# A fused attention and MLP kernel: sums of exponentials by narrow products, the maximum of phi as a tree, q of four units transposed on the tensor engine, and low parts moved from VectorE to GpSimd

## The chip, the cores and the metric

The kernel runs on one core of a Trainium2 chip. The metric is the time of one execution in device microseconds (us), the median of three runs. Engines are called as the profile calls them: PE (the tensor engine's products; PEld its weight loads), DVE (VectorE), ACT (ScalarE), POOL (GpSimd) and SP (SyncE, which issues all transfers here).

## The reference

```
q, k, v: 4 x 8 x 576 x 64     phi: 4 x 8 x 576 x 32        (batch, heads, seq, dim)
a = exp(phi - max over seq);  a = a / (sum over seq + 1e-9)
k_m = a^T k;  v_m = a^T v                                   (32 x 64 per head)
scores = q k_m^T / 8;  attn = softmax over the 32
x = attn v_m, heads side by side                            (2304 x 512)
h = max(x w1, x w2, x w3);  x = h w_out                     (512 -> 768 -> 512)
y = x w_in;  out = softplus(y) w_out2                       (512 -> 2048 -> 512)
```

## The kernel before

Every float32 operand of a large product is split into a high part `hi` (the value cast to the matmul's float32r) and a low part `lo` (the value minus `hi`); a product is then three, hi·hi, lo·hi and hi·lo. The weights arrive as 64-bit floats, two 32-bit words each; the class `Conv` (lines 255 to 290) turns them into float32 with one ACT and two DVE steps, then makes `hi` by a cast and `lo` by a subtraction. `hi_eng` and `lo_eng` say on which engines; the defaults are ACT and POOL.

Attention goes by eight units `u`, each a batch and four heads. `load_phi` brings phi as 128 rows by 4 heads by 5 row groups by 32; the fifth group has only 64 rows, so its other 64 are filled (table `pad`). `att_max` (L349) reduces over the row groups on DVE, PE transposes the result, DVE takes the maximum over rows, PE spreads it. `att_exp` subtracts it and takes exponentials on ACT. `att_sum` (L371) adds `et` over the row groups on DVE; `sums` (L398) adds over rows by one product with ones, and its reciprocal `ri` scales k_m and v_m when ACT copies them out of PSUM (`kvd`). `att_x` multiplies `et` with k or v in twenty products of 32 output rows (L387, L389). `att_tr` turns k_m and v_m by products with selection matrices. `att_q` (L472) transposes q by one DVE instruction of 128 x 1152, in 32 x 32 blocks; a second form, on PE, is there for units named in `qpe`, which is empty. `att_sc` makes the scores, `att_sm0` to `att_sm2` the softmax, and `att_fin` turns the result back and splits it into `ah` and `al`.

The MLP follows: `u_mm` multiplies v_m with w1 to w3 (so x is never formed) and splits the result into `uh` and `ul`; `m1` multiplies by the attention weights and takes the maximum of three (L602 to L609); `hsplit` splits h into `hh` and `hlo` (table `hl` gives the engine of the low part); `m1out` multiplies by w_out (L643 to L645), 12 products of 384 columns for each split piece. `y0_split` splits the first half's result. All of this is done for two halves of the batch. The last stage (L863 to L908) does the second MLP.

What sets the order: `PLAN` is a list of steps for units 0 to 3 and the first weights; for the rest the table `C` gives the slot at which each step is written beside the main loop. From what is written, the framework's scheduler makes one fixed order for each engine; an engine takes its instructions strictly in that order. In the profile the plan runs to about 94 us, the first half's m1 to 174, its m1out to 222, the second half's m1 to 291 and its m1out to 343.

Of the kernel before, what the change touches and what calls it, by code (L numbers as in the profile page):

```python
# [165 lines left out]
def fused_kernel(ctx: ExitStack, tc: tile.TileContext, q, k, v, phi, w1, w2, w3, w_out, m_in, m_out, out):  # L166
# [201 lines left out]
    def att_sum(u):  # L368
        d = U[u]
        er = t_p.tile([P, 4 * M], F32, tag="mx", name="er", bufs=2)  # L370
        nc.vector.tensor_reduce(out=er, in_=d["et"].rearrange("p r c -> p c r"), op=ALU.add, axis=AX.X)  # L371
        d["er"] = er

    def att_x(u, i):
# [6 lines left out]
        if new_ri and u < 4:  # L381
            sums(u, pst()[:, 0:2])
        for r in range(R4 + 1):
            for h in range(4):
# [1 line left out]
                if r < R4:
                    nc.tensor.matmul(xp[a, 0:D], et[:, r, a], x[:, h, r], start=(r == 0), stop=False)  # L387
                else:
                    nc.tensor.matmul(xp[a, 0:D], et[0:SREM, r, a], xr[:, h], start=False, stop=True)  # L389
        if new_ri and u >= 4:  # L390
            sums(u, xp[:, 64:66])
# [3 lines left out]

    def sums(u, s):
        d = U[u]
        nc.tensor.matmul(s, d.pop("er"), ones, start=True, stop=True)  # L398
        ri = t_p.tile([P, 1], F32, tag="ri", name="ri", bufs=2)
        nc.vector.tensor_scalar(out=ri, in0=s[:, 0:1], scalar1=1e-9, scalar2=None, op0=ALU.add)  # L400
        nc.vector.reciprocal(out=ri, in_=ri)
        d["ri"] = ri
# [559 lines left out]
```

## Time and profile before

| | us |
|---|---|
| median of three runs (747.47 to 751.0) | 749.6 |
| the profiled execution | 749.13 |
| its span | 747.3 |
| busy: PE / DVE / ACT / POOL | 697.7 / 475.4 / 307.6 / 245.5 |

The span is the time from the first to the last instruction; the execution's own time is 1.8 us longer. Busy time is a sum over stretches with different limits, so the prediction goes by stretch. Ends of matmuls are modelled: a PE that is shown busy may still run below its peak.

### The profile page before, as it was taken

Reading aid. Unit: us, or ns where it says so; the run is one execution under the profiler, and the core shown is the slowest. Engines: PE = TensorE matmul, PEld = TensorE weight load, DVE = VectorE, ACT = ScalarE, POOL = GpSimd, SP = SyncE. Lnnn points to the kernel's source line nnn. Section 1 sums busy time; section 2 is a strip of 40 time slices with the busy share of each in tenths; the row PEclk is TensorE's granted clock in tenths of the full one; section 3 lists DMA queues with packets and bytes.
Section 4 is the critical chain, followed back from the end, with each engine's and each line's share of the span. In section 5 each row is a group of like instructions: output and inputs, shape, how many; then the busy total and the mean of one; then the engine's idle time right before and its main releaser. Section 6 shows DMA issues by size and latency. Waiting matters only on the chain. (4 is left out here: it accounts for less than half of the span.)

```text
span 747.3 us, 11707 instructions
## 1 busy us (share of the span) xinstructions
PE 697.7 (93%) x4380; PEld 628.2 (84%) x4380; DVE 475.4 (64%) x858; ACT 307.6 (41%) x645; POOL 245.5 (33%) x237
## 2 busy tenths in 40 slices
PE   2679799999989999998999999999999999999997
PEld 1457588889889999987899889898889899898896
DVE  7799978999978984882333487333784334433343
ACT  2256456644657763652333453222542223222221
POOL 1212301333675413642222363222552223422221
PEclk9979789999999999998999999999999999999999
DMA  9993703341252400540000032000241000011112
GB/s 291 289 305 123 222 13 109 120 131 54 78 162 85 128 1 7 165 146 24 1 1 1 7 127 93 0 1 1 64 133 30 1 1 0 1 43 42 43 43 84
DMA packets 52568, 59.21 MB, mean 79 GB/s; under 512 B 8992, under 2 KB 46368, under 8 KB 52512
## 3 DMA queue, kind: packets, MB, share of 16 engines
q1 hardware_dynamic: 52512, 58.47, 25.5%
q8 instruction: 34, 0.56, 0.3%
q14 instruction: 22, 0.18, 0.1%
HBM read 53.74 MB, written 4.72 MB: 78 GB/s over the span
## 5 line engine op out<-in xcount | busy, mean ns | idle before, releaser
L250 POOL TENSOR_TENSOR gl<-m,gh 128x384 fp32r<-128x384 f32 x96 | 100.4, 1047 | 259.3 <-ACT gh L242 242.6
L869 DVE TENSOR_SCALAR e<-pst 128x384 int32<-128x384 int32 x96 | 53.2, 554 | 138.7 <-PE pst L863 138.7
L871 ACT ACTIVATE L<-e 128x384 f32<-128x384 f32 x96 | 50.3, 524 | 188.2 <-DVE e L869 188.1
L895 PE MATMUL acc<-oh,gh 128*128 128x512 f32 x288 | 114.2, 396 | 0.4 <-ACT gh L242 0.4
L895 PE MATMUL acc<-ol,gh 128*128 128x512 f32 x288 | 113.8, 395 | 0.0
L863 PE MATMUL pst<-yb,ih 128*128 128x384 f32 x384 | 102.1, 336 | 0.0
L873 DVE SCALAR_TENSOR_TENSOR m<-pst,L 128x384 f32<-128x384 f32 x96 | 53.4, 556 | 57.9 <-ACT L L871 56.8
L602 PE MATMUL psm<-ah,uh 128*128 128x288 f32 x288 | 86.9, 312 | 2.7 <-ACT kT L436 1.7
L602 PE MATMUL psm<-al,uh 128*128 128x288 f32 x288 | 85.8, 299 | 0.0
L602 PE MATMUL psm<-ah,ul 128*128 128x288 f32 x288 | 84.3, 300 | 0.0
L895 PE MATMUL acc<-oh,gl 128*128 128x512 f32 x288 | 82.7, 394 | 0.0
L242 ACT ACTIVATE gh<-m 128x384 fp32r<-128x384 f32 x96 | 50.0, 523 | 62.8 <-DVE m L873 60.8
L863 PEld LDWEIGHTS pst<-yb,ih 128*128 128x128 f32 x384 | 70.0, 188 | 3.4 <-DVE m L873 0.7
L863 PE MATMUL pst<-y0h,ih 128*128 128x384 f32 x192 | 65.7, 342 | 3.9 <-DVE m L873 3.8
L863 PE MATMUL pst<-y0l,ih 128*128 128x384 f32 x192 | 65.3, 340 | 0.0
L863 PE MATMUL pst<-y0h,il 128*128 128x384 f32 x192 | 65.2, 340 | 0.0
L250 POOL TENSOR_TENSOR wl<-cg,wh 128x384 fp32r<-128x384 f32 x37 | 39.8, 1080 | 75.5 <-ACT wh L242 63.1
L863 PE MATMUL pst<-yb,il 128*128 128x384 f32 x192 | 64.4, 335 | 0.0
L895 PEld LDWEIGHTS acc<-oh,gh 128*128 128x128 f32 x288 | 54.3, 189 | 10.7 <-ACT gh L242 0.9
L895 PEld LDWEIGHTS acc<-oh,gl 128*128 128x128 f32 x288 | 53.6, 187 | 11.4
L895 PEld LDWEIGHTS acc<-ol,gh 128*128 128x128 f32 x288 | 54.3, 188 | 9.0
L602 PEld LDWEIGHTS psm<-ah,uh 128*128 128x128 f32 x288 | 54.7, 194 | 6.2 <-ACT kT L436 2.0
(142 smaller groups left out, 1410.9 us busy)
## 6 DMA issues: line engine op xcount, KB each, us to landing
wraw<-in_moe_w_dram SPq DMA_DIRECT2D x66, 256.0 KB, 3.6
raw<-in_moe_w_in_dram SPq DMA_DIRECT2D x16, 512.0 KB, 3.5
raw<-in_moe_w_out_dram SPq DMA_DIRECT2D x16, 512.0 KB, 3.6
qr<-in_q_dram SPq DMA_DIRECT2D x8, 576.0 KB, 4.6
out_dram<-o SPq DMA_DIRECT2D x18, 256.0 KB, 2.1
kvm<-in_k_dram SPq DMA_DIRECT2D x8, 512.0 KB, 7.9
kvm<-in_v_dram SPq DMA_DIRECT2D x8, 512.0 KB, 7.6
wor<-in_moe_w_out_dram SPq DMA_DIRECT2D x6, 512.0 KB, 3.5
```

Of the source, the lines that this page charges most:

```text
L242: nc.scalar.activation(out=dst, in_=src, func=AF.Copy)
L250: e.tensor_tensor(out=dst, in0=src, in1=hi, op=ALU.subtract)
L602: nc.tensor.matmul(x, l[:, t, ws], r[:, cs], start=(n == 0), stop=(n == 5))
L863: nc.tensor.matmul(hx, l[:, ds], r[:, cs], start=(n == 0), stop=(n == 3 * ND - 1))
L869: nc.vector.tensor_scalar(out=e.bitcast(I32), in0=hx.bitcast(I32), scalar1=0x7FFFFFFF, scalar2=None, op0=ALU.bitwise_and)
L871: nc.scalar.activation(out=L, in_=e, func=AF.Softplus, scale=-1.0)
L873: nc.vector.scalar_tensor_tensor(out=m, in0=hx, scalar=0.0, in1=L, op0=ALU.max, op1=ALU.add)
L895: nc.tensor.matmul(acc[0][t], l[:, t * P:(t + 1) * P], r, **kw)
```

## The change

Five edits. (1) `att_sum` and `sums` go; after the first of a unit's two sets of products, `att_x` issues twenty more with the same weights `et` and two columns of ones, into columns 64 and 65 of the same PSUM tile. (2) `att_max` takes maxima of halves in three two-input operations in place of one reduction. (3) `qpe` names units 0 to 3: q is loaded as k is, in two transfers, and transposed by 20 products with the identity, then copied out of PSUM by ACT; k_m is turned by two products in place of eight, and the scores are made by products of 64 output rows. (4) All tables of engines for high and low parts go: every `Conv` has its high part on ACT and its low part on POOL; all `hlo` but the first and last of a half are on POOL, and so are two more `al`. (5) The pad of phi is a POOL memset to 0, and the zero fill of `et` goes.

```diff
-    ('ca', 0, 1, {'lo_eng': 'pool', 'hi_eng': 'act'}),
-    ('ex', 0, 'dve'),
-    ('sm', 0),
+    ('ca', 0, 1),
+    ('ex', 0),
...
-    'esub': ['pool', 'pool', 'pool', 'dve'],
-    'wok': [{'hi_eng': 'act'}, {'lo_eng': 'dve', 'hi_eng': 'act'}, {'lo_eng': 'pool', 'hi_eng': 'dve'}, {'hi_eng': 'act', 'lo_eng': 'pool'}, {'lo_eng': 'pool', 'hi_eng': 'act'}, {'lo_eng': 'dve', 'hi_eng': 'dve'}],
-    'al': ['dve', 'dve', 'pool', 'dve'],
+    'al': ['pool', 'pool', 'pool', 'dve'],
-    'hl': ['pool', 'pool', 'dve', 'pool', 'pool', 'dve', 'dve', 'dve', 'pool', 'dve', 'dve', 'pool', 'dve', 'pool', 'pool', 'dve', 'dve', 'pool'],
+    'hl': ['dve'] + ['pool'] * 16 + ['dve'],
-    'qpe': (),
-    'pad': ['act', 'act', 'dve', 'act', 'act', 'act', 'dve', 'pool'],
-    'zed': ['dve', 'pool', 'dve', 'pool', 'pool', 'pool', 'dve', 'pool'],
+    'qpe': (0, 1, 2, 3),
...
-        cast(C["pad"][u], ph[SREM:P, :, R4, :], ph[SREM:P, :, 0, :])
+        nc.gpsimd.memset(ph[SREM:P, :, R4, :], 0.0)
...
-        nc.vector.tensor_reduce(out=mx, in_=d["ph"].rearrange("p h r m -> p h m r"), op=ALU.max, axis=AX.X)
+        ph = d["ph"]
+        m2 = t_p.tile([P, 4, 2, M], F32, tag="m2", name="m2", bufs=1)
+        nc.vector.tensor_tensor(out=m2, in0=ph[:, :, 0:2], in1=ph[:, :, 2:4], op=ALU.max)
+        nc.vector.tensor_tensor(out=mx, in0=m2[:, :, 0], in1=m2[:, :, 1], op=ALU.max)
+        nc.vector.tensor_tensor(out=mx[0:SREM], in0=mx[0:SREM], in1=ph[0:SREM, :, R4], op=ALU.max)
...
-        (nc.vector if C["zed"][u] == "dve" else nc.gpsimd).memset(et[SREM:P, R4], 0.0)
...
-        er = t_p.tile([P, 4 * M], F32, tag="mx", name="er", bufs=2)
-        nc.vector.tensor_reduce(out=er, in_=d["et"].rearrange("p r c -> p c r"), op=ALU.add, axis=AX.X)
...
+        if new_ri:
+            for r in range(R4 + 1):
+                for h in range(4):
+                    a = slice(32 * h, 32 * h + 32)
+                    k = slice(0, P if r < R4 else SREM)
+                    nc.tensor.matmul(xp[a, D:D + 2], et[k, r, a], ones[k], start=(r == 0), stop=(r == R4))
+            ri = t_p.tile([P, 1], F32, tag="ri", name="ri", bufs=2)
+            nc.vector.tensor_scalar(out=ri, in0=xp[:, D:D + 1], scalar1=1e-9, scalar2=None, op0=ALU.add)
+            nc.vector.reciprocal(out=ri, in_=ri)
...
-        nc.tensor.matmul(s, d.pop("er"), ones, start=True, stop=True)
...
-                nc.tensor.matmul(sc[64 * s:64 * s + 64, 0:HS], kT[:, s], qT[:, s, c * HS:(c + 1) * HS],
+                o = s ^ units[u][0] % 2
+                nc.tensor.matmul(sc[64 * s:64 * s + 64, 0:HS], kT[:, o], qT[:, o, c * HS:(c + 1) * HS],
                                  start=True, stop=True)
...
-                c = w_conv(i, p, **C["wk"].get((i, p), {}))
+                c = w_conv(i, p)
```

The scheduler's fixed orders move with it. On DVE at the start of the program, before (qT is the transposed q, mx and er the reductions, mc and md the maximum over rows, ph and et phi and its exponentials):

```order
L472 STREAM_TRANSPOSE qT<-qr 128x2x18x32
L349 TENSOR_REDUCE mx<-ph 128x128 x2
L472 STREAM_TRANSPOSE qT<-qr 128x2x18x32
L353 TENSOR_REDUCE mc<-psm 128x1 x2
L355 TENSOR_SCALAR md<-ident,mc 128x128 x2
L362 TENSOR_TENSOR ph<-ph,psm 128x640 x2
L365 MEMSET et 64x128
L371 TENSOR_REDUCE er<-et 128x128
```

and DVE at the same place with the change:

```order
L342 TENSOR_TENSOR m_128<-ph 128x256
L343 TENSOR_TENSOR mx<-m_128 128x128
L344 TENSOR_TENSOR mx<-mx,ph 64x128
L342 TENSOR_TENSOR m_140<-ph 128x256
L343 TENSOR_TENSOR mx<-m_140 128x128
L344 TENSOR_TENSOR mx<-mx,ph 64x128
L348 TENSOR_REDUCE mc<-psm 128x1
L350 TENSOR_SCALAR md<-ident,mc 128x128
L348 TENSOR_REDUCE mc<-psm 128x1
L350 TENSOR_SCALAR md<-ident,mc 128x128
L357 TENSOR_TENSOR ph<-ph,psm 128x640 x2
```

Nothing stands between the two maxima and the subtractions any more, and no sum follows them. On POOL at the end of the first half's m1out and after it, before (sT are steps of the softmax, al and hlo low parts of attention and of h, wl of weights, y0l of the first half's result):

```order
L250 TENSOR_TENSOR hlo<-h,hh 128x384
L250 TENSOR_TENSOR wl<-cg,wh 128x384 x2
L250 TENSOR_TENSOR hlo<-h,hh 128x384
L250 TENSOR_TENSOR y0l_2887<-ya,y0h_2886 128x384
L250 TENSOR_TENSOR y0l_3014<-ya,y0h_3013 128x384
L250 TENSOR_TENSOR y0l_3166<-ya,y0h_3165 128x384
L250 TENSOR_TENSOR y0l_3314<-ya,y0h_3313 128x384
L250 TENSOR_TENSOR wl<-cg,wh 128x384
L250 TENSOR_TENSOR hlo<-h,hh 128x384
L250 TENSOR_TENSOR wl<-cg,wh 128x384
```

and POOL there with the change:

```order
L503 TENSOR_TENSOR sT<-sT,ssm 128x576
L241 TENSOR_TENSOR al<-aT,ah 128x576
L241 TENSOR_TENSOR y0l_3117<-ya,y0h_3116 128x384 x3
L241 TENSOR_TENSOR y0l_3244<-ya,y0h_3243 128x384 x2
L241 TENSOR_TENSOR y0l_3396<-ya,y0h_3395 128x384 x2
L241 TENSOR_TENSOR y0l_3544<-ya,y0h_3543 128x384 x2
L241 TENSOR_TENSOR y0l_3244<-ya,y0h_3243 128x384
L241 TENSOR_TENSOR y0l_3396<-ya,y0h_3395 128x384
L241 TENSOR_TENSOR y0l_3544<-ya,y0h_3543 128x384
L241 TENSOR_TENSOR wl<-cg,wh 128x384 x2
L241 TENSOR_TENSOR hlo<-h,hh 128x384
```

The twelve low parts of the first half's result now stand in one piece, ahead of the next low parts of weights. On PE after the first unit's products, before (kvd is the scaled k_m or v_m, psm and pst are PSUM tiles):

```order
L428 MATMUL psm<-pick,kvd 32x128 x8
L351 MATMUL psm<-ident,mx 128x128
L485 MATMUL psm<-qT,kT 128x288 x4
L387 MATMUL psm<-kvm,et 32x64 x12
```

and PE there with the change (qn and qnr are q as loaded):

```order
L382 MATMUL psm<-ones,et 32x2 x20
L399 MATMUL psm<-pick_90,kvd 64x128 x2
L346 MATMUL psm<-ident,mx 128x128
L450 MATMUL psm<-ident,qn 64x128 x8
L453 MATMUL psm<-ident,qnr 64x64 x2
L450 MATMUL psm<-ident,qn 64x128 x8
L453 MATMUL psm<-ident,qnr 64x64
L351 MATMUL psm<-md,onesq 128x128
L453 MATMUL psm<-ident,qnr 64x64
L470 MATMUL psm<-qT,kT 64x288 x4
```

The sums and the transposes of q stand ahead of the first scores; the transposes of two more units follow before the first product of `u_mm`.

## Rows read from the trace of the kernel before

**Rows 1.** Busy time by stretch: PE, PEld, DVE, ACT, POOL, PEclk, DMA, GB/s.

```profile
0.00:42.00 42.00, 19.05 (x237) 13.04 (x238) 33.27 (x62) 11.85 (x26) 8.68 (x23) 0.99 1.06 295
42.00:94.00 52.00, 43.23 (x540) 33.16 (x540) 50.23 (x101) 26.70 (x63) 13.66 (x16) 0.83 0.70 205
94.00:174.00 80.00, 77.50 (x643) 69.54 (x644) 71.25 (x153) 45.23 (x109) 16.80 (x19) 0.97 0.32 99
174.00:222.00 48.00, 43.80 (x237) 42.28 (x236) 45.19 (x71) 25.75 (x54) 29.77 (x23) 0.96 0.29 94
222.00:291.00 69.00, 67.99 (x492) 67.56 (x492) 55.28 (x117) 43.74 (x102) 22.40 (x21) 1.00 0.18 58
291.00:343.00 52.00, 47.36 (x256) 45.33 (x256) 38.92 (x55) 28.68 (x55) 28.84 (x21) 0.96 0.38 122
343.00:747.00 404.00, 398.76 (x1983) 357.27 (x1981) 181.30 (x302) 125.59 (x238) 125.35 (x114) 1.00 0.10 33
```

**Rows 2.** Waits of PE over the span: total us, times, longest.

```profile
PE psm L351 <- DVE mx L349: 14.5, 3, 9.0
...
PE psm L643 <- DVE ul L585: 3.4, 1, 3.4
...
PE psm L645 <- POOL hlo L250: 1.0, 1, 1.0
```

**Rows 3.** Timeline of DVE: start, us; 0 to 105 and 190 to 215 us.

```profile
4.84 2.33 DVE L472 STREAM_TRANSPOSE qT<-qr 128x1152 f32<-128x1152 f32 x1 [1.28 <-DMA qr<-in_q_dram]
...
31.78 2.30 DVE L472 STREAM_TRANSPOSE qT<-qr 128x1152 f32<-128x1152 f32 x1
...
194.59 0.52 DVE L250 TENSOR_TENSOR hlo<-h,hh 128x384 fp32r<-128x384 f32 x1
...
197.43 1.37 DVE L250 TENSOR_TENSOR hlo<-h,hh 128x384 fp32r<-128x384 f32 x1
```

**Rows 4.** Groups of DVE to 222 us: busy, mean ns; idle before.

```profile
L371 DVE TENSOR_REDUCE er<-et 128x128 f32<-128x640 f32 x8 | 10.1, 1265 | 0.1
...
L349 DVE TENSOR_REDUCE mx<-ph 128x128 f32<-128x640 f32 x8 | 10.0, 1258 | 0.5 <-ACT ph L242 0.5
...
L250 DVE TENSOR_TENSOR hlo<-h,hh 128x384 fp32r<-128x384 f32 x9 | 8.1, 908 | 0.0
...
L250 DVE TENSOR_TENSOR wl<-cg,wh 128x384 fp32r<-128x384 f32 x7 | 3.8, 547 | 0.1
...
L250 DVE TENSOR_TENSOR wol<-cg,woh 128x256 fp32r<-128x256 f32 x4 | 1.6, 404 | 0.0
...
L246 DVE CAST wh<-cg 128x384 fp32r<-128x384 f32 x8 | 3.1, 390 | 0.0
...
L276 DVE SCALAR_TENSOR_TENSOR cg<-wraw,cg 128x384 int32<-128x384 int32 x31 | 21.1, 689 | 0.3
```

**Rows 5.** Groups of POOL to 222 us.

```profile
L250 POOL TENSOR_TENSOR wl<-cg,wh 128x384 fp32r<-128x384 f32 x22 | 23.2, 1061 | 57.8 <-ACT wh L242 45.3 <-DVE wh L246 7.6 <-DVE ri L400 2.8
...
L250 POOL TENSOR_TENSOR hlo<-h,hh 128x384 fp32r<-128x384 f32 x9 | 11.0, 1227 | 8.3 <-ACT hh L242 5.4 <-PE psm L485 1.8 <-PE psm L645 1.1
...
L250 POOL TENSOR_TENSOR y0l<-ya,y0h 128x384 fp32r<-128x384 f32 x8 | 10.9, 1389 | 0.0
```

**Rows 6.** Timeline of POOL, 190 to 215 us.

```profile
196.85 1.53 POOL L250 TENSOR_TENSOR hlo<-h,hh 128x384 fp32r<-128x384 f32 x1
```

**Rows 7.** Timeline of PE, 33 to 42 us; each product has two records.

```profile
33.16 0.65 PE L428 MATMUL psm<-pick,kvd 128*32 128x128 f32 x16 [0.43 <-ACT kvd L393]
...
34.31 2.21 PE L485 MATMUL psm<-qT,kT 128*128 128x288 f32 x8 [0.50 <-ACT kT L433]
...
36.66 0.65 PE L387 MATMUL psm<-kvm,et 128*32 128x64 f32 x32
...
40.03 0.44 PE L412 MATMUL psm<-pick,kvd 128*64 128x128 f32 x4
```

**Rows 8.** Groups of ACT to 222 us.

```profile
L242 ACT ACTIVATE wh<-cg 128x384 fp32r<-128x384 f32 x21 | 10.9, 521 | 10.3 <-DVE cg L276 7.5 <-PE psm L575 2.5
```

More of the change, by code (lines that the diff above doesn't have):

```diff
@@ L30 @@
     ('wl', 0, 0),
-    ('ca', 0, 1, {'lo_eng': 'pool', 'hi_eng': 'act'}),
-    ('ex', 0, 'dve'),
-    ('ex', 1, 'dve'),
-    ('sm', 0),
+    ('ca', 0, 1),
+    ('ex', 0),
+    ('ex', 1),
     ('ld', 0, 0),
-    ('sm', 1),
     ('ax', 0, 0),
-    ('ca', 0, 0, {'lo_eng': 'pool', 'hi_eng': 'dve'}),
+    ('ca', 0, 0),
     ('tr', 0, 0),
@@ L44 @@
     ('qT', 0),
-    ('ca', 0, 2, {'lo_eng': 'pool', 'hi_eng': 'dve'}),
+    ('ca', 0, 2),
     ('cb', 0, 0),
@@ L53 @@
     ('ld', 0, 1),
-    ('qT', 1, 'dve'),
+    ('qT', 1),
     ('tr', 1, 0),
@@ L60 @@
     ('ld', 3, 1),
-    ('ca', 0, 3, {'lo_eng': 'pool', 'hi_eng': 'act'}),
+    ('ca', 0, 3),
     ('mx', 3),
@@ L64 @@
     ('ax', 0, 1),
-    ('ex', 2, 'dve'),
+    ('ex', 2),
     ('s2', 0, 'pool'),
@@ L70 @@
     ('s0', 1),
-    ('ex', 3, 'pool'),
+    ('ex', 3),
     ('s1', 1, 'dve'),
@@ L77 @@
     ('wl', 1, 0),
-    ('ca', 1, 1, {'lo_eng': 'dve', 'hi_eng': 'dve'}),
+    ('ca', 1, 1),
     ('fin', 0, 'dve'),
@@ L83 @@
     ('u', 0, 3, (0,)),
-    ('sm', 2),
     ('s2', 1, 'pool'),
@@ L87 @@
     ('wl', 2, 0),
-    ('qT', 3, 'dve'),
+    ('qT', 3),
     ('ax', 2, 1),
-    ('ca', 1, 0, {'lo_eng': 'dve', 'hi_eng': 'act'}),
+    ('ca', 1, 0),
     ('wl', 2, 1),
-    ('ca', 1, 3, {'lo_eng': 'pool', 'hi_eng': 'dve'}),
-    ('sm', 3),
+    ('ca', 1, 3),
     ('wl', 3, 0),
@@ L105 @@
     ('tr', 3, 1),
-    ('ca', 1, 2, {'lo_eng': 'dve', 'hi_eng': 'act'}),
+    ('ca', 1, 2),
     ('u', 1, 1, (0, 1)),
@@ L109 @@
     ('u', 1, 3, (0, 1)),
-    ('ca', 2, 0, {'lo_eng': 'pool', 'hi_eng': 'act'}),
+    ('ca', 2, 0),
     ('u', 1, 0, (0, 1)),
     ('cb', 1, 2),
-    ('ca', 2, 1, {'lo_eng': 'pool', 'hi_eng': 'dve'}),
+    ('ca', 2, 1),
     ('u', 0, 1, (1,)),
@@ L122 @@
     ('m1', 1, 0, 0),
-    ('ca', 2, 3, {'lo_eng': 'pool', 'hi_eng': 'act'}),
+    ('ca', 2, 3),
     ('u', 0, 3, (1,)),
@@ L131 @@
     ('s0', 3),
-    ('ca', 2, 2, {'lo_eng': 'pool', 'hi_eng': 'act'}),
+    ('ca', 2, 2),
     ('cb', 2, 2),
@@ L154 @@
     'w8l': 17,
-    'wk': {(4, 0): {'hi_eng': 'act', 'lo_eng': 'dve'}, (4, 1): {'lo_eng': 'dve', 'hi_eng': 'act'}, (3, 0): {'hi_eng': 'dve', 'lo_eng': 'pool'}, (5, 3): {'lo_eng': 'pool'}, (3, 1): {'hi_eng': 'act', 'lo_eng': 'dve'}, (5, 0): {'hi_eng': 'dve', 'lo_eng': 'pool'}, (4, 2): {'lo_eng': 'pool'}, (3, 2): {'hi_eng': 'act', 'lo_eng': 'dve'}, (5, 1): {'lo_eng': 'pool', 'hi_eng': 'act'}, (5, 2): {'lo_eng': 'pool', 'hi_eng': 'act'}, (4, 3): {'hi_eng': 'dve', 'lo_eng': 'pool'}},
     'wo_off': {(4, 0): 1, (5, 3): 0, (5, 1): -1, (3, 3): -1, (3, 0): 0, (4, 1): -2, (3, 2): 0, (5, 0): -1, (3, 1): 1, (5, 2): -2, (4, 3): 0, (4, 2): 0},
-    'hl': ['pool', 'pool', 'dve', 'pool', 'pool', 'dve', 'dve', 'dve', 'pool', 'dve', 'dve', 'pool', 'dve', 'pool', 'pool', 'dve', 'dve', 'pool'],
+    'hl': ['dve'] + ['pool'] * 16 + ['dve'],
     'us0': 1,
     'us1': 0,
-    'qpe': (),
-    'pad': ['act', 'act', 'dve', 'act', 'act', 'act', 'dve', 'pool'],
-    'zed': ['dve', 'pool', 'dve', 'pool', 'pool', 'pool', 'dve', 'pool'],
+    'qpe': (0, 1, 2, 3),
 }
@@ L357, in att_max, with att_exp @@
         d["ma"] = st[:, P:2 * P].rearrange("p (h m) -> p h m", h=4)
-    def att_exp(u, sub="dve"):
+    def att_exp(u):
         d = U[u]
@@ L364, in att_exp @@
         nc.scalar.activation(out=et.rearrange("p r h m -> p h r m"), in_=ph, func=AF.Exp)
-        (nc.vector if C["zed"][u] == "dve" else nc.gpsimd).memset(et[SREM:P, R4], 0.0)
         d["et"] = et.rearrange("p r h m -> p r (h m)")
-    def att_sum(u):
-        d = U[u]
-        er = t_p.tile([P, 4 * M], F32, tag="mx", name="er", bufs=2)
-        nc.vector.tensor_reduce(out=er, in_=d["et"].rearrange("p r c -> p c r"), op=ALU.add, axis=AX.X)
-        d["er"] = er
     def att_x(u, i):
@@ L380, in att_x @@
         new_ri = "ri" not in d
-        if new_ri and u < 4:
-            sums(u, pst()[:, 0:2])
         for r in range(R4 + 1):
@@ L385, in att_x @@
                 a = slice(32 * h, 32 * h + 32)
[L386 to L391, printed above, removed]
+                k = slice(0, P if r < R4 else SREM)
+                nc.tensor.matmul(xp[a, 0:D], et[k, r, a], x[:, h, r] if r < R4 else xr[:, h], start=(r == 0), stop=(r == R4))
+        if new_ri:
+            for r in range(R4 + 1):
+                for h in range(4):
+                    a = slice(32 * h, 32 * h + 32)
+                    k = slice(0, P if r < R4 else SREM)
+                    nc.tensor.matmul(xp[a, D:D + 2], et[k, r, a], ones[k], start=(r == 0), stop=(r == R4))
+            ri = t_p.tile([P, 1], F32, tag="ri", name="ri", bufs=2)
+            nc.vector.tensor_scalar(out=ri, in0=xp[:, D:D + 1], scalar1=1e-9, scalar2=None, op0=ALU.add)
+            nc.vector.reciprocal(out=ri, in_=ri)
+            d["ri"] = ri
         kvd = t_p.tile([P, D], F32, tag="kvd", name="kvd", bufs=3)
@@ L394, in att_x @@
         d["xp", i], d["kvd", i] = xp, kvd
-    def sums(u, s):
-        d = U[u]
-        nc.tensor.matmul(s, d.pop("er"), ones, start=True, stop=True)
[L399 to L402, printed above, removed]
     def att_tr(u, i):
@@ L730, in fused_kernel @@
             nc.gpsimd.memset(x[:, 2 * s + 1 - s % 2].bitcast(F32), 0.0)
-    STEPS = dict(ph=load_phi, ld=load_x, q=load_q, mx=att_max, ex=att_exp, sm=att_sum, ax=att_x, tr=att_tr, qT=att_q,
+    STEPS = dict(ph=load_phi, ld=load_x, q=load_q, mx=att_max, ex=att_exp, ax=att_x, tr=att_tr, qT=att_q,
                  sc=att_sc, s0=att_sm0, s1=att_sm1, s2=att_sm2, fin=att_fin, wl=w_load, ca=conv_a, cb=conv_b,
@@ L752, in fused_kernel @@
         u = 4 + n
-        for sl, fn in zip(C["att"][n], (lambda u=u: att_max(u), lambda u=u: att_exp(u, C["esub"][u - 4]), lambda u=u: att_sum(u),
+        for sl, fn in zip(C["att"][n], (lambda u=u: att_max(u), lambda u=u: att_exp(u), lambda: None,
                                         lambda u=u: (att_kv(u), load_u(u + 2) if u + 2 < 8 else None),
@@ L759, in wo_go @@
         def wo_go(j=j):
-            wcv[j] = wo_conv(j, **C["wok"][j])
+            wcv[j] = wo_conv(j)
             wcv[j][0].a()
```

## The prediction

> **What bounds the kernel now.** I read three views: busy time by stretch, the waits of the tensor engine (PE), and the groups of instructions of the vector engine (DVE). By stretch [rows 1], the last 404 us are PE's alone: 398.8 us busy at a granted clock of 1.00, the other engines under half. The change touches nothing there, so the question is the first 343 us. From 42 to 222 us DVE is the fullest engine: 50.2 of 52, 71.3 of 80 and 45.2 of 48 us, 166.7 of 180 together, while PE leaves at least 8.8 + 2.5 + 4.2 = 15.5 us idle (a lower bound, since ends of matmuls are modelled) and is granted 0.83 of its clock in the 52 us after 42, where it ran in pieces. From 222 to 343 us PE leads again (68.0 of 69 us, then 47.4 of 52). The first 42 us are full of transfers: DMA share 1.06 at 295 GB/s, PE busy 19.1. The waits say the same: before the last stage PE waits longest for DVE's maximum of phi, 14.5 us in three waits, and then for a PSUM buffer that DVE had not yet read, 3.4 us in one [rows 2]. So work taken off DVE should help from 42 to 222 us, if nothing else takes its place.
>
> **What leaves DVE.** Four of eight transposes of q go: 4 x 2.32 = 9.3 us, all before 35 us (the first starts at 4.84, the fourth at 31.78 [rows 3]). Eight sums `er` go: 8 x 1.265 = 10.1 [rows 4]. Eight reductions `mx` of 1.258 become three maxima of 256, 128 and (64 partitions) 128 elements. The nearest row is a two-input operation of 256 elements, 0.404 us; at 0.40 + 0.27 + 0.23 = 0.90 (the shorter two are my estimate from it) the tree saves 8 x 0.36 = 2.9 us; at three times 0.404 it saves only 0.4, and if the shorter two cost 0.15 each, 4.4. Casts to ACT: 8 x 0.390 and 4 of 256 elements at about 0.28 (0.390 scaled by length) give 4.2. Low parts to POOL: 7 x 0.547 + 4 x 0.404 + 7 of the 9 `hlo` before 222 us at 0.908 + two `al` at about the same make 3.8 + 1.6 + 6.4 + 1.8 = 13.6. Five fills of pads and zeros go, put at 0.25 each (a cast of three times their length takes 0.390): 1.3. Sum: 9.3 + 10.1 + 2.9 + 4.2 + 13.6 + 1.3 = **41.4 us**, of which I place some 15 before 42 us (four transposes, a quarter of the sums, half the trees and fills, a fifth of the casts).
>
> **What the low parts cost on POOL.** There `wl` takes 1.061 and `hlo` 1.227 us [rows 5]: 7 x 1.06 + 4 x 0.7 + 7 x 1.23 + 2 x 1.4 = 21.6 us more POOL before 222 us, and 7 more `hlo`, 8.6 us, behind it. POOL has room on average (13.7 of 52, 16.8 of 80 us), least from 174 to 222 (29.8 of 48 [rows 1]). But DVE slows beside POOL. Within 3 us of one timeline the same `hlo` takes 0.52 us at 194.59, before POOL starts, and 1.37 at 197.43 [rows 3], beside a subtraction that POOL began at 196.85 and that took 1.53 [rows 6]. The means show how often: the conversion's 31 L276 average 0.689, against 0.547 for the equally long `wl`, and the nine `hlo` 0.908 against 0.52 [rows 3, 4]. That is 31 x 0.14 + 9 x 0.39 = 7.9 us for POOL's 68.9 us up to 222 us [rows 1]; these are about half of DVE's forms of the kind, so I take 0.25 us of DVE for each of POOL's, so 21.6 us of it give back 5.4 (bounds 0 and 21.6). Net for the low parts 8.2 us, and for DVE 41.4 - 5.4 = 36.0, of which some **21 after 42 us**.
>
> The Trainium skill, SBUF — State Buffer, section "Who interferes with whom", states more: POOL and a DVE instruction with two inputs in SBUF exclude each other for a whole instruction, and a reduction never takes part. By that rule the low parts could cost DVE all the 21.6 us that POOL spends on them, more than the 13.6 they free, and the tree gives up a form that was immune; the rows agree in kind (POOL's subtraction ended at 198.38, 0.95 after the second `hlo` began, and 0.95 + 0.52 is near its 1.37), but their means show it only now and then. It is a rival below.
>
> **What PE gets.** Twenty sums of two columns a unit repeat the weights of the twenty products beside them, sixteen of which take 0.65 us at 64 columns [rows 7]: 20 x 0.65 / 16 = 0.8 a unit, 6.5 in all (less if fewer columns cost less, twice that at the lower of the two clocks: bounds 3 and 13). The eight wide sums that go give back some 0.3 each (0.44 for two products [rows 7]), 2.4; net +4, of which 3 after 42 us. Twenty transposes a unit for four units: the nearest rows are eight products of 32 columns in 0.65 us, four side by side, and two of 64 columns in 0.44. Sixteen in eight pairs and four short ones make 2.6 us at the first rate and 3.7 at the second, so 10.4 to 15 us; the scores of these units go from four products of full width, 2.2 us, to two pairs, between 1.1 and 2.2, so 0 to 4.4 us back; turning k takes two products in place of eight, 0.2 us back a unit. This is all early work: three of the four units stand before the first product of u in PE's new order, and PE is idle 23 of the first 42 us. I cost it at nothing; were it all on the path, +10.
>
> **What ACT and the queues get.** Twelve casts at 0.52 or less and, for four units, two copies of 512 columns and one of 128 out of PSUM: 5.8 us and, at 0.52 x 512 / 384 = 0.7 and 0.3 us [rows 8], 6.8. ACT is busy 26.7 of 52 and 45.2 of 80 us [rows 1], so I cost this at nothing; each low part now waits for ACT's cast ahead of it, and a late cast holds POOL's whole queue. On SP the four q loads become two transfers each, 512 and 64 KB in place of 576, at the same place in line: same bytes, so 0 (bounds 0 and 2, the length of one such load, 576 KB at 295 GB/s, on the first). The pads become POOL memsets that wait for a buffer of phi, not for the transfer; phi's maximum no longer waits for a pad.
>
> **The sum.** Up to 42 us the transfers set the pace; DVE's 15 us there buy 2.5 (bounds 0 and 6: phi's maximum is 2.3 us earlier without the transpose ahead of it). From 42 to 222 us relief is 21 us. PE can return its 15.5 us idle and some of what the 0.83 clock lost (0.17 x 52 = 8.8). Casts and copies on ACT, which end about as many of PE's waits as DVE, keep part. I take 12.5 (bounds 0 and 21). PE's sums take 3 back. Behind 174 us POOL's longer queue takes 1 (bounds 0 and 16, below). So 2.5 + 12.5 - 3 - 1 = 11 us. The profiled execution took 749.1 us, 1.8 around its span of 747.3, and lies 0.5 below the median of the runs. 749.1 - 11 = **738 us**.
>
> **The rivals.**
> *POOL becomes the queue (slower).* From 174 to 222 us its load goes from 29.8 to some 29.8 + 7 x 1.23 + 2 x 1.4 + 2 x 0.7 = 42.6 of 48 us, with `sT` steps that wait for DVE and ACT standing between `hlo`s that PE needs; and in its new order the twelve low parts of y0 stand in one piece, 12 x 1.39 = 16.7 us [rows 5], ahead of the next weights' low parts, where before four stood ahead (5.6). PE, nearly full there, would wait up to 11 us for the weights less what it can do without them: 8 taken; `hlo`s late from 174 to 222 cost 4, and from 291 to 343, with 28.8 + 8.6 of 52 us on POOL, another 4. That is 749.1 - 15 + 3 + 16 = 753 us. It decides once POOL falls more than the two prepared steps of h behind PE. Against it: PE's waits on POOL are now 1 us in all the kernel [rows 2].
> *Exclusion.* If POOL blocks DVE for all of its added 21.6 us, relief falls from 36.0 to 19.8, after 42 us to about 5; 3 of it come back: 749.1 - 2.5 - 3 + 3 + 1 = 748, no change.
> *DVE's relief was hidden anyway.* From 94 to 174 us PE is 97% busy and before 42 the transfers rule: gain 3, against PE's +3: 749. For it speaks that stretch; against it the 8.8 and 4.2 us beside it.
> *All of it counts.* 21 + 6 - 3 = 24 us: 725. For it DVE at 93% over 180 us; against it PE's 15.5 us.
>
> **How the numbers follow.** A difference of 0.5%, 3.7 us, is about what a measurement of this kernel can tell. Forecast (730 to 745): 0.44; all of it: 0.14; together faster by over 0.5%: 0.58. Exclusion 0.09 and hidden 0.12: within 0.5%, 0.21. POOL's queue: slower, 0.21. The range 724 to 754 leaves out the far halves of the two outer cases, some 0.2.
>
> **What would show it.** Right: DVE from 42 to 222 us falls to about 80% busy though the stretch is shorter, PE's wait for phi's maximum shrinks below 10 us, the first long run of L602's successor starts 2 to 4 us earlier, and the last stage of 404 us keeps its length. The forecast is wrong where PE's largest wait reads POOL `hlo` or `wl`, where DVE's conversion (0.689) goes above 0.9 us, where the transposes of q stand on PE after 60 us, or where PE's idle time from 42 to 222 us stays above 15 us with DVE no longer full.

## The result, and the profile after

The change is slower: 754.3 us against 749.1, ratio 1.0059, 95% interval 1.0045 to 1.0074. The forecast was 738, faster. The profiled execution of the changed kernel took 757.9 us (span 756.0), 3.6 above its median; a second one (e16 below, span 750.0) lies 2.5 below it, and both are used.

By stretch, the columns as in [rows 1], cut at the same places of the work (m1out of half one from 172, m1 of half two from 221, its m1out from 301):

```profile
0.00:42.00 42.00, 21.92 (x284) 15.36 (x286) 17.77 (x53) 13.25 (x23) 9.16 (x26) 0.97 1.04 265
42.00:100.00 58.00, 50.46 (x840) 37.69 (x837) 49.37 (x108) 34.29 (x77) 15.68 (x18) 0.91 0.72 206
100.00:172.00 72.00, 72.00 (x674) 64.75 (x673) 54.11 (x127) 45.62 (x108) 23.07 (x25) 0.98 0.30 93
172.00:221.00 49.00, 48.80 (x286) 45.69 (x279) 36.95 (x60) 22.18 (x48) 29.03 (x25) 1.00 0.23 73
221.00:301.00 80.00, 74.46 (x497) 72.04 (x496) 62.37 (x124) 50.72 (x114) 33.57 (x31) 0.94 0.25 77
301.00:351.00 50.00, 45.98 (x252) 43.55 (x251) 34.88 (x48) 28.73 (x55) 34.71 (x27) 0.99 0.43 127
351.00:756.00 405.00, 398.87 (x1982) 357.19 (x1981) 181.42 (x302) 125.63 (x238) 126.19 (x115) 1.00 0.10 33
```

DVE did nearly what was forecast: 158.2 us busy up to 221 us against 199.9 [rows 1], though some 7 of these 41.7 us only moved behind 221 us, where DVE has 62.4 us for 55.3. PE became dense from 100 to 221 us. The time was lost ahead of 100 us and, most of it, from 221 to 301 us, where 69 us of m1 became 80. The longest wait of PE over the span, and the waits for ACT and POOL that bear on the loss (`ya` is m1out's result as copied out of PSUM, `mt` the first step of m1's maximum of three):

```profile
PE psm L346 <- DVE mx L344: 11.3, 2, 8.9
...
PE psm L590 <- ACT ya L233: 2.1, 1, 2.1
PE psm L633 <- POOL hlo L241: 1.9, 3, 0.9
PE psm L590 <- ACT mt L594: 1.8, 1, 1.8
```

The maximum of phi [rows 2] gave back 3.2 us. New are two waits for ACT, at 223 and 229 us. ACT's timeline shows why (L514 is unit 6's and 7's `ah`):

```profile
218.13 0.69 ACT L493 ACTIVATE sT<-sT 128x576 f32<-128x576 f32 x1 [4.19 <-DVE sT L492]
220.91 0.69 ACT L514 ACTIVATE ah<-aT 128x576 fp32r<-128x576 f32 x1 [2.10 <-DVE aT L509]
224.17 0.68 ACT L514 ACTIVATE ah<-aT 128x576 fp32r<-128x576 f32 x1 [2.57 <-DVE aT L509]
224.76 0.85 ACT L233 ACTIVATE ya<-psm 128x384 f32<-128x384 f32 x2
225.72 5.07 ACT L233 ACTIVATE y0h<-ya 128x384 fp32r<-128x384 f32 x12
230.70 0.39 ACT L594 ACTIVATE mt<-psm 128x288 f32<-128x288 f32 x1
```

and before, at the same place of the work:

```profile
199.52 0.69 ACT L526 ACTIVATE ah<-aT 128x576 fp32r<-128x576 f32 x1 [0.46 <-DVE aT L521]
...
202.23 1.77 ACT L242 ACTIVATE y0h<-ya 128x384 fp32r<-128x384 f32 x4 [0.31 <-DVE al L250]
...
210.95 1.33 ACT L242 ACTIVATE y0h<-ya 128x384 fp32r<-128x384 f32 x3
...
223.13 1.35 ACT L242 ACTIVATE y0h<-ya 128x384 fp32r<-128x384 f32 x3
```

The last `ah` of the softmax comes 24.7 us later. `ya`, for whose PSUM buffers PE waits, stands behind it in ACT's queue. And y0 lies in the room of the softmax's tiles (its pool opens when theirs closes), so no y0h can start before the last `al`; the twelve then come at once, and `mt` stands behind them. Between the two waits, at about 227 us, PE's clock falls to its lower level, and it stays there through the second, some 10 us in all:

```profile
222.00:226.00 4.00, 1.89 (x14) 1.66 (x14) 1.93 (x4) 1.72 (x4) 1.32 (x1) 1.00 0.00 0
226.00:230.00 4.00, 3.33 (x15) 2.93 (x13) 0.57 (x2) 4.00 (x11) 3.67 (x4) 0.61 0.72 252
230.00:234.00 4.00, 2.86 (x12) 2.86 (x13) 2.77 (x5) 3.94 (x9) 4.00 (x5) 0.50 0.03 10
234.00:238.00 4.00, 4.00 (x19) 3.85 (x19) 3.97 (x8) 3.69 (x8) 4.00 (x4) 0.61 0.45 135
238.00:242.00 4.00, 4.00 (x32) 4.00 (x31) 3.81 (x9) 2.01 (x4) 4.00 (x5) 1.00 0.46 131
```

The softmax is late because unit 4's scores are. In PE's timeline before, and after:

```profile
146.81 0.65 PE L485 MATMUL pst<-qT,kT 128*128 128x288 f32 x2
```

```profile
183.76 2.10 PE L473 MATMUL pst<-qT,kT 128*128 128x288 f32 x8
```

In PE's fixed order they stood behind 306 of the first half's 432 products of m1, and now stand behind all of them and 60 of m1out.

### The profile page after: what moved, and what is told of

It reads as the page before. It is cut to its first block, busy times and chain, and to the rows that moved or that the text cites. A ratio compares the mean times of both kernels' runs of the same rounds, so it can differ in the third digit from the quotient of the medians.

```text
span 756.0 us, 12561 instructions
## 1 busy us (share of the span) xinstructions
PE 712.5 (94%) x4796; PEld 636.3 (84%) x4796; DVE 436.9 (58%) x818; ACT 320.4 (42%) x662; POOL 271.4 (36%) x266
## 5 line engine op out<-in xcount | busy, mean ns | idle before, releaser
L859 ACT ACTIVATE L<-e 128x384 f32<-128x384 f32 x96 | 50.3, 524 | 187.0 <-DVE e L857 186.7
L883 PE MATMUL acc<-oh,gh 128*128 128x512 f32 x288 | 114.2, 396 | 0.4 <-ACT gh L233 0.4
L883 PE MATMUL acc<-ol,gh 128*128 128x512 f32 x288 | 113.9, 395 | 0.0
L883 PE MATMUL acc<-oh,gl 128*128 128x512 f32 x288 | 82.7, 394 | 0.0
L241 POOL TENSOR_TENSOR wl<-cg,wh 128x384 fp32r<-128x384 f32 x44 | 46.4, 1059 | 85.0 <-ACT wh L233 75.7
L266 DVE TENSOR_SCALAR cg<-cg 128x384 int32<-128x384 int32 (+2 forms) x88 | 46.5, 530 | 32.2 <-ACT cg L265 16.5
L851 PE MATMUL pst<-y0l,ih 128*128 128x384 f32 x192 | 64.9, 338 | 0.0
L851 PE MATMUL pst<-yb,il 128*128 128x384 f32 x192 | 64.4, 335 | 0.0
L883 PEld LDWEIGHTS acc<-oh,gh 128*128 128x128 f32 x288 | 54.3, 189 | 10.6 <-ACT gh L233 0.9
L883 PEld LDWEIGHTS acc<-oh,gl 128*128 128x128 f32 x288 | 53.6, 187 | 11.4
```

The lines of the kernel that those rows point to most:

```text
L241: e.tensor_tensor(out=dst, in0=src, in1=hi, op=ALU.subtract)
L266: nc.vector.tensor_scalar(out=gi, in0=gi, scalar1=3, scalar2=None, op0=ALU.logical_shift_left)
L851: nc.tensor.matmul(hx, l[:, ds], r[:, cs], start=(n == 0), stop=(n == 3 * ND - 1))
L859: nc.scalar.activation(out=L, in_=e, func=AF.Softplus, scale=-1.0)
L883: nc.tensor.matmul(acc[0][t], l[:, t * P:(t + 1) * P], r, **kw)
```

## The experiments

Stages in us, read from the start of one product to the next: **front** to the 108th product of m1; **m1** to the 432nd; **m1out** to its last product of hi·hi (L643 in the kernel before) in half one, which stands up to 1 us ahead of its last product of all; **m1b** to the 864th of m1; **turn** to the first product of the last stage's second matrix (L895 in the kernel before, L883 with the change), then **rest** to the end. One profiled execution each; median and ratio (to the kernel before on the same chip) are of repeated runs. The medians come from several chips, on which the kernel before differs by up to 1.2 us, so small differences between rows are better read from the ratios.

| kernel | median | ratio, interval | front | m1 | m1out | m1b | turn | rest | last ah |
|---|---|---|---|---|---|---|---|---|---|
| before | 749.1 | 1 | 101.7 | 72.3 | 47.6 | 69.7 | 52.1 | 403.9 | 199.5 |
| change | 754.3 | 1.0059 (1.0045-1.0074) | 106.9 | 63.8 | 50.2 | 79.8 | 50.7 | 404.6 | 224.2 |
| e16 change again | 751.8 | one run | 103.4 | 63.8 | 50.2 | 79.3 | 49.5 | 403.8 | 220.7 |
| e1 early softmax | 745.9 | 0.9956 (0.9930-0.9982) | 103.0 | 67.6 | 53.7 | 65.2 | 49.5 | 403.2 | 202.0 |
| e15 the same | 746.7 | 0.9962 (0.9946-0.9977) | 103.3 | 67.6 | 53.5 | 65.3 | 51.4 | 403.1 | 202.0 |
| e2 y0l on DVE | 752.8 | 1.0048 (1.0027-1.0068) | 105.6 | 63.8 | 50.2 | 78.7 | 49.8 | 403.4 | 222.8 |
| e17 y0h in pieces | 752.8 | 1.0046 (1.0029-1.0062) | 106.7 | 63.8 | 50.2 | 78.1 | 50.7 | 404.0 | 224.0 |
| e3 q on DVE | 755.6 | 1.0073 (1.0040-1.0106) | 100.9 | 64.3 | 50.4 | 79.3 | 50.0 | 403.4 | 218.9 |
| e4 tree alone | 757.1 | 1.0104 (1.0074-1.0134) | 102.4 | 64.9 | 49.5 | 82.7 | 52.2 | 403.6 | 219.1 |
| e13 late alone | 751.3 | 1.0035 (1.0021-1.0048) | 101.7 | 64.4 | 50.9 | 77.6 | 52.8 | 404.2 | 217.7 |
| e5 e1, q on DVE | 754.7 | 1.0076 (1.0046-1.0105) | 108.3 | 68.1 | 54.1 | 68.1 | 50.3 | 404.5 | 208.3 |
| e6 e1, low back | 750.7 | 1.0033 (1.0016-1.0051) | 99.6 | 69.4 | 52.3 | 70.7 | 52.5 | 403.5 | 199.6 |
| e7 e1, q and low back | 751.8 | 1.0046 (1.0027-1.0066) | 100.4 | 69.7 | 52.5 | 69.5 | 52.7 | 404.2 | 199.8 |
| e10 e1, sums on DVE | 751.7 | 1.0034 (1.0014-1.0055) | 101.8 | 69.4 | 48.5 | 74.6 | 49.8 | 406.2 | 212.7 |
| e11 e1, max reduce | 747.3 | 0.9982 (0.9966-0.9997) | 105.7 | 68.5 | 49.7 | 68.6 | 50.1 | 404.0 | 202.4 |
| e12 e1, plan low back | 747.0 | 0.9983 (0.9965-1.0001) | 99.0 | 69.7 | 50.6 | 68.8 | 51.2 | 404.4 | 197.6 |
| e8 e4, early | 752.8 | 1.0041 (1.0020-1.0061) | 107.2 | 68.1 | 51.3 | 69.8 | 52.7 | 404.2 | 203.3 |
| e14 before, e1's slots | 756.7 | 1.0093 (1.0070-1.0116) | 104.5 | 69.0 | 55.0 | 70.9 | 51.3 | 404.0 | 205.9 |
| e9 hlo alone | 756.1 | 1.0096 (1.0079-1.0113) | 102.2 | 72.3 | 57.2 | 68.9 | 51.3 | 403.3 | 200.1 |

**e1, early softmax**, the changed kernel with other slots; a negative slot s of `scs` is slot 20 + s of the loop before:

```diff
-    'att': [..., [13, 13, 15, 15, 15], [15, 18, 19, 21, 21]],
-    'scs': [[4, 4, 4, 4, 5, 6], [5, 5, 5, 6, 6, 7], [6, 6, 6, 7, 10, 10], [8, 11, 12, 13, 14, 18]],
+    'att': [..., [12, 12, 13, 13, 13], [13, 14, 15, 15, 15]],
+    'scs': [[-4, -4, -4, -3, -2, 1], [-3, -2, -2, -1, 0, 2], [-1, 0, 1, 1, 2, 4], [2, 3, 4, 5, 6, 8]],
```

> The changed kernel, but the attention of units 6 and 7 and the softmax steps of units 4 to 7 are written some slots earlier, so that the first scores of unit 4 stand among the products of m1 in place of behind 60 products of m1out. All up to 100 us has the order of the changed kernel. Theory L (the softmax of unit 7 ends late, its last al at 225.6 us, and the room of y0 is the room of these softmax tiles, so that all twelve y0h and y0l come in one piece while PE starts the second half): the last al ends near 200 us, the y0h stand in three pieces, PE's waits of 2.1 us for ya and 1.8 us for mt go, the clock stays at 2.4 GHz from 221 us on, the second half's m1 takes 70 to 73 us in place of 80, and the time is 743 to 748 us. Theory P (POOL's load of low parts holds the weights): POOL has the same work, so the second half still loses half of it or more: 750 to 755 us.

Theory L held: last `ah` at 202.0, m1b 65.2 us (some 2 of it because 18 of the second half's products of m1 now stand ahead of it, among m1out's, where the kernel before has two), PE full and its clock whole:

```profile
224.00:290.00 66.00, 66.00 (x479) 65.92 (x478) 54.42 (x115) 42.18 (x97) 22.82 (x21) 1.00 0.20 61
```

It beats the kernel before by 0.4% and the change by more.

**e2, y0l on DVE** (`rest("pool", ...)` of `y0_split` becomes `"dve"`).

> The changed kernel, but the twelve low parts of y0 are made by DVE in place of POOL; ACT's twelve y0h stay in one piece. Theory P (the 13.2 us of y0l on POOL hold the low parts of the weights): POOL is free at 226 us, wl comes 13 us earlier, and the second half's m1 falls from 80 to 72 us or less: 745 to 748 us. Theory L (the bunch on ACT and its late start do it): PE's waits for ya (2.1 us) and for mt (1.8 us) stay, the clock still falls, the time stays at 752 to 757 us, or rises by up to 3 us because DVE's low parts, 12 x 0.55 us, stand ahead of its maxima.

POOL's run of y0l is gone and m1b is 78.7: that run was not the cause. The run itself was there, as forecast, 13.19 us ahead of `wl`, but PE never waited for `wl`.

**e3, q on DVE** (`'qpe': ()` in the changed kernel).

> The changed kernel, but q of units 0 to 3 is loaded in one transfer and transposed by DVE, as before. Theory F (the front lost 5 us through the transposes of q on PE at the low clock, the copies of them on ACT and the later transfers): the first product of u starts within 2 us of the 41.9 us of the kernel before (50.1 with the change), the first long run of m1 near 95 us in place of 100, and the time is 747 to 751 us if the late softmax of the second half stays. The rival, that the front lost through the order of the transfers and the sums alone: the first product of u stays behind 47 us and the time within 753 to 757 us.

The first product of u started at 51.4 us, not 44: theory F fell, and the time is the rival's. The profiled execution had a short front; the median is that of the change.

**e4, tree alone**, the kernel before with edit (2) and the pad's memset.

> The kernel before, with nothing changed but phi's maximum as a tree and the pad as a POOL memset of 0. Theory S (the order is made by the scheduler from slots that fit the kernel before and no other, so that any edit ahead of 100 us sends the scores of unit 4 behind m1): the first scores of unit 4 start after 180 us (154 before), the last al ends past 215 us, and the time is 752 to 757 us although DVE has 3 us less to do. The rival (each edit costs or gives what it does by itself): the tree frees 2 to 3 us of DVE where PE waits for phi's maximum: 746 to 749 us.

Theory S held in kind: unit 4's scores start at 178.6 us (it said after 180), m1b is 82.7 and the time 757.1 us, by one edit of 8 x 1 us. PE's longest wait in m1b is another than the change's, 7.8 us in three for DVE's `ul`, the low part of u.

**e5, e6, e7, e8**: e1 with `'qpe': ()`; with the tables `wk`, `wok`, `hl`, `al` and the plan's `ca` options of before; with both; and e4 with e1's slots.

> The kernel with the early softmax (745.9 us), but with q of units 0 to 3 loaded in one transfer and transposed by DVE. Theory F (the transposes of q on PE, their copies on ACT and the later transfers cost the front 4 to 5 us, which the second half's own loss hid in the earlier run): the first long run of m1 starts by 94 us and the time is 740 to 743 us. The rival (DVE's 9.3 us are worth what PE and ACT pay for them): 745 to 748 us.

> The kernel with the early softmax (745.9 us), but with the tables of engines for high and low parts as before (weights of u and of w_out, hlo, al). The forecast's step (moving them to ACT and POOL frees DVE 13.6 + 4.2 us at a cost of 5.4 for the slower DVE beside POOL, where PE waits for DVE): 748 to 752 us. The rivals (PE no longer waits for DVE, or POOL holds up DVE for as long as it is freed): 744 to 747 us, with DVE busier by 10 us or more up to 222 us and PE's waits as they were.

> The kernel with the early softmax (745.9 us), with both q and the low parts as before, so that of the change only the sums on PE, the tree of maxima and the pads are left. If the two edits' costs add up: the sum of the differences that the two runs beside this one show against 745.9 us. The forecast's terms for what is left (DVE freed of 10.1 and 2.9 us, PE's sums 3 to 6 us): 743 to 748 us.

> The kernel before with the tree of maxima and the pads alone (757.1 us), and with the slots that bring the softmax of units 4 to 7 forward. Theory S (the tree cost nothing by itself, its 8 us were the late softmax): the first scores of unit 4 again stand among the products of m1, the second half's m1 takes 70 to 73 us in place of 83, and the time is 745 to 749 us. The rival (the tree or its memset on POOL costs by itself): 752 us or more.

With the softmax early m1b is 68 to 71 us in all four. With e1's slots the low parts back cost 4.8 us against e1, as the forecast's step had it (748 to 752). The rest surprised: q on DVE costs 8.8 us, outside both expectations (theory F fell a second time), and both together 5.9, not 13.6: the edits don't add up. e8 got its m1b back (69.8 for 82.7) but only 4.3 us of the 8, so that its time is the rival's (752 or more): its front was 107.2, for 102.4 in e4.

**e9, hlo alone**, the kernel before with one row of a table:

```diff
-    'hl': ['pool', 'pool', 'dve', ...
+    'hl': ['dve'] + ['pool'] * 16 + ['dve'],
```

> The kernel before with one table changed: all hlo but the first and the last of a half on POOL. The order keeps the scores of unit 4 among the products of m1. Rival of the forecast (POOL becomes the queue: hlo late on POOL cost 4 us from 174 to 222 and 4 from 291 to 343): 752 to 757 us, with PE's waits on POOL hlo above 4 us. What the runs so far suggest (at the start of the last stage PE waits 2.1 us for DVE's m with hlo on POOL, 3.4 to 4.2 with hlo on DVE, and its clock then falls to 0.83 to 0.91): the last stage is 2 to 3 us shorter, PE's waits on POOL stay under 2.5 us, and the time is 745 to 748 us.

As slow as the POOL rival said, 756.1 us, all of it in m1out (57.2 for 47.6), but PE does not wait for hlo. The waits from 170 to 235 us are

```profile
PE psm L643 <- DVE ya L246: 4.9, 2, 3.8
PE psm L643 <- ACT ya L242: 3.9, 2, 3.0
```

and DVE's timeline has, since hlo left it, four conversions in a row ahead of `ya`:

```profile
206.56 2.21 DVE L275 TENSOR_SCALAR cg<-cg 128x384 int32<-128x384 int32 x2 [1.39 <-ACT cg L272]
208.69 2.61 DVE L276 SCALAR_TENSOR_TENSOR cg<-wraw,cg 128x384 int32<-128x384 int32 x2
211.23 2.38 DVE L275 TENSOR_SCALAR cg<-cg 128x512 int32<-128x512 int32 x2
213.53 2.88 DVE L276 SCALAR_TENSOR_TENSOR cg<-raw,cg 128x512 int32<-128x512 int32 x2
```

Two things meet here. `ya` stands behind these eight instructions, where in the kernel before it stood between them. And POOL, which has the hlo now, is busy 11.9 of the 12 us from 204 to 216, and each of the eight takes 1.1 to 1.5 us; in the kernel before, the 384-column ones that POOL left alone take 0.35 (L275) and 0.55 us (L276). What each of the two is worth was not taken apart.

**e10, e11, e12**: e1 with edit (1) undone (the zero fill of `et` is back with it); with (2) and (5) undone for phi; with the plan's `ca` options of before.

> The kernel with the early softmax (745.9 us), but with the sums of exponentials by DVE and one product, as before. Forecast's term (DVE's 8 x 1.265 us lie where PE waits for DVE, and PE's narrow products cost 3 to 6 us): 747 to 752 us. The rival (they are worth what they cost): 744 to 747 us.

> The kernel with the early softmax (745.9 us), but with phi's maximum as one reduction and the pads as casts, as before. Forecast's term (2.9 us of DVE and the pads' 1.3 us, of which PE gets about a half): 746 to 749 us. The rival (at a place where the transfers rule they are worth nothing): 744 to 746 us.

> The kernel with the early softmax (745.9 us), but with the engines of the weights' high and low parts as before in the plan alone (twelve conversions up to 100 us); all later ones stay moved. Theory G (in the plan ACT and POOL are what PE waits for, and the move there costs the front 3 to 5 us; the runs with the low parts as before reached the 108th product of m1 at 99.6 and 100.4 us, those with them moved at 103 to 108): that product starts by 101 us and the time is 740 to 743 us. The rival (the spread of the front is the clock of single executions): 744 to 748 us.

Sums back on DVE cost 5.8 us, but 9.4 of m1b come with a softmax that is late again (212.7), so the sums' own worth stays open. The tree with its pads is worth 1.4, with intervals that overlap. With the plan's high and low parts as before the front is 99.0 us, as theory G said; the time, 747.0, is the rival's, since m1b and turn gave 5.3 us back.

**e13, late alone**, the kernel before with one dependency, a copy of one element:

```diff
+        if u == 4:
+            nc.vector.tensor_copy(qT[0:1, 0, 0:1], h_t[5][0:1, TOK - 1:TOK])
         nc.vector.transpose(out=qT.rearrange("x a (p j) -> x a j p", j=NJB), in_=qr...
```

> The kernel before, but the transpose of unit 4's q waits for one element of the last h of the first half (a DVE copy of one element ahead of it), so that its scores come behind 60 products of m1out, as with the change; all edits of the change are absent. Theory L (late softmax alone): from the 108th product of m1 to the end of the first m1out 113 to 116 us in place of 120, the second half's m1 79 to 83 us in place of 70, PE waiting for ya or mt behind a run of twelve y0h, the time 752 to 757 us. The rival (the second half's loss needs POOL's or ACT's added work of the change): second half's m1 under 74 us and 744 to 750 us.

It reproduces the change's middle with no edit of it: m1 -7.9, m1out +3.3, m1b +7.9 us (the change: -8.5, +2.6, +9.9). The run of twelve is there too, but the wait behind it is another: PE waits 2.9 us for DVE's `ul`, not for `ya` or `mt`. ACT's timeline, PE's, and the clock:

```profile
219.30 5.08 ACT L242 ACTIVATE y0h<-ya 128x384 fp32r<-128x384 f32 x12 [0.25 <-issue]
```

```profile
226.96 0.66 PE L576 MATMUL psm<-wh,vh 128*128 128x384 f32 x1 [2.91 <-DVE ul L587]
```

```profile
228.00:232.00 4.00, 4.00 (x17) 3.87 (x17) 4.00 (x7) 2.79 (x8) 4.00 (x4) 0.50 0.02 4
```

Its time, 751.3, is under the 752 expected: alone, the late softmax costs 0.35%, where the change costs 0.59%. The profiled execution is the longest of its runs, 2.0 us above the median, so that its stages show the loss somewhat too large.

**e14, e15, e16**: the kernel before with e1's slots; e1 again; the change again.

> The kernel before with the moved slots of the version with the early softmax and nothing of the change. If the slots alone make that version fast: 744 to 747 us. If they only restore what the kernel before had by its own slots, and the gain is the change's: 748 to 752 us.

> The changed kernel with the early softmax, once more, with more rounds: 744 to 748 us, ratio to the kernel before 0.993 to 0.998. A ratio of 0.998 or above would take back that it beats the kernel before.

> The changed kernel once more, for its profile alone. If the front's 5 us are in its order, the 108th product of m1 starts at 106 to 108 us again; if they are the clock of single executions, anywhere from 101 to 107 us. The second half's m1 takes 78 to 82 us either way.

The slots alone make the kernel before slower by 0.9% (m1out 55.0), outside both expectations; so the gain of e1, which e15 repeats, belongs to the edits and slots together. Read the other way: at the old slots the edits cost 0.6%, at e1's they gain 1.4% (1.0093 to 0.9956). e16's front is 103.4 us with the order that took 106.9.

**e17, y0h in pieces**, the changed kernel, eight y0h waiting for an h of half two:

```diff
+        n = NCH * dm + c
+        if n >= 4:
+            nc.vector.tensor_copy(y0[dm][0][0:1, c * CH:c * CH + 1], h_t[jof(NJ if n < 8 else NJ + 1)][0:1, TOK - 1:TOK])
```

> The changed kernel with the softmax as late as in it and the same order on PE; only the last eight of the twelve y0h wait, four at a time, for one element of an h of the second half (a DVE copy of one element ahead of each), so that neither ACT nor POOL has them in one piece. If the run of twelve holds PE: the wait of 1.8 us for mt goes, the wait of 2.1 us for ya stays, the clock is low for 6 us or less in place of 11, the second half's m1 takes 72 to 75 us in place of 80, and the time is 746 to 750 us. If the late ya and ah do it: 77 us or more, and 752 to 757 us.

The second wait went and the clock was low for about 3.5 us in place of 10, yet m1b is 78.1 and the time 752.8, as the second expectation had it. At the 480th product of m1 this run was 2.5 us ahead of the change, at the 540th no more. Between the two PE waits 1.6 us for something that the profile does not show:

```profile
241.00:251.00 10.00, 8.37 (x58) 7.79 (x57) 9.90 (x23) 9.07 (x22) 7.46 (x7) 1.00 0.29 99
```

```profile
PE psm L590 <- issue: 1.6, 1, 1.6
```

So splitting the run, by itself, does not give m1b back. What remains, that y0's split falls into m1b at all and that `ya` is late, was not taken apart further.

## Why the prediction was wrong

**The account.** Mean of the change's two executions against before: front +3.5, m1 -8.5, m1out +2.6, m1b +9.9, turn -2.0, rest +0.3, together +5.7; the medians say +5.2. In e13, without the change, the three middle stages make +3.3 of the change's +4.0, in an execution 2.0 us above its median. That the late softmax costs m1b its length is shown both ways (e13 and e4 bring it in, e1 and e8 take it out); by the ratios it is somewhat over half of the loss (0.35 of 0.59%), and the rest is not assigned.

**The step that failed** is "From 42 to 222 us relief is 21 us. [...] I take 12.5": it priced DVE's relief as if all else kept its place in the orders. The relief came (41.7 us up to 221, or 34.6 without the work that moved behind it, where 36.0 net were forecast). With the scores pushed behind it bought next to nothing: m1 and m1out together take 114.0 us in the change and 115.3 in e13, where DVE is relieved of nothing, and PE is nearly full in both. From the 108th to the 864th product of m1 the kernel before takes 189.6 us, the change 193.8 and 193.3, e1 186.5, and e14, the kernel before with e1's slots, 194.9. So the edits together cost 4 us at the old slots, gain 8.4 at e1's, and 3.1 where each kernel has slots that suit it: what DVE's relief buys depends on the order, and the sum had one number for it. How much of the 8.4 is DVE's relief stays open; e6 says that the low parts have a part in it. The rival that DVE's relief was hidden is nearest in its reason (PE was 97% busy in m1 and is full there now) and in its gain of 3; its 749 us was not met.

**What made it slower** no rival named. The POOL rival had the place, the sign, 753 us and 8 of the 10 us, by luck, for its cause was wrong: the twelve y0l in one piece, which the orders showed, were the sign that the softmax ends late, and were read as a price on POOL (e2 takes it away: 1.1 us). Its 4 us from 291 to 343 had the wrong sign: with hlo off DVE the turn is 1.4 and 2.6 us shorter (49.5 to 51.4 us in all twelve such executions, 51.3 to 52.8 in the seven others), PE waiting 2.1 for DVE's m in place of 3.4, with its clock less low (before, then e16):

```profile
330.00:350.00 20.00, 16.61 (x74) 15.12 (x73) 10.04 (x19) 7.11 (x14) 3.45 (x4) 0.83 0.22 75
```

```profile
335.00:355.00 20.00, 17.90 (x92) 15.88 (x91) 10.33 (x18) 9.00 (x17) 6.12 (x6) 1.00 0.28 83
```

**The front**: -2.5 forecast. The six executions of the changed front (change, e16, e1, e15, e2, e17) took 103.0 to 106.9 us, the three of very nearly the order before (before, e9, e13) 101.7 to 102.2, and the two with q, sums and tree changed but the plan's high and low parts as before (e6, e12) 99.6 and 99.0. That suggests that the other edits gave about the 2.5, and that the plan's casts on ACT ("I cost this at nothing") and low parts on POOL took 4 or more. It does not show it: e3 and e5, the same edits in the front, took 100.9 and 108.3, so that single executions differ by more than this. Which wait does it was not tried.

**Mis-sized terms.** From the groups of DVE and of PE up to 222 us:

```profile
L342 DVE TENSOR_TENSOR m<-ph 128x256 f32<-128x256 f32 x8 | 4.3, 543 | 8.1 <-DMA ph<-in_phi_dram 8.0
L344 DVE TENSOR_TENSOR mx<-mx,ph 64x128 f32<-64x128 f32 x8 | 3.3, 411 | 0.2
L343 DVE TENSOR_TENSOR mx<-m 128x128 f32<-128x128 f32 x8 | 2.3, 282 | 0.2
```

```profile
L450 PE MATMUL psm<-ident,qn 128*64 128x128 f32 x128 | 13.6, 368 | 0.0
L453 PE MATMUL psm<-ident,qnr 64*64 64x64 f32 x32 | 3.9, 289 | 0.0
```

The tree takes 9.9 us where the reductions took 10.0 [rows 4]: 0.1 saved, not 2.9. Left alone its three steps take 0.42, 0.28 and 0.28 us, 0.98 in all, near the 0.90 forecast; but beside POOL one of the eight first steps takes 1.41 us, and two of the last 0.74 and 0.89. The transposes of q took 17.5 us, above the bound of 15. The sums took 7.5 for 6.5.

**Exclusion** shows in single instructions, and not in the mean. DVE's conversion, two inputs, L267, averages 0.683 us (31 of them) against 0.689 [rows 4], though POOL was busy 76.9 us up to 221 for 68.9. But the 22 of them that POOL hardly overlaps take 0.53 to 0.56 us, and the nine that it overlaps by half or more 1.01 on average (in the kernel before 20 at 0.55 and seven at 1.14). DVE's timeline with the change, once beside a POOL instruction (50.10 to 51.37 us) and once alone:

```profile
50.48 1.31 DVE L267 SCALAR_TENSOR_TENSOR cg<-wraw,cg 128x384 int32<-128x384 int32 x1
...
62.04 0.55 DVE L267 SCALAR_TENSOR_TENSOR cg<-wraw,cg 128x384 int32<-128x384 int32 x1
```

The rule of the Trainium skill, SBUF — State Buffer, "Who interferes with whom", that DVE's two-input operations and POOL hold each other up, agrees with these instructions. The rival priced it for every us that POOL added, and so often they do not meet. In the tree, which gave up a reduction for three two-input operations, and in e9 it did cost.
